# The first four head pairs of a forgetting-attention and SwiGLU kernel: q and k in two parts, gate sums by TensorE, 38 products of the identity at the start, a new order of the loads

## The chip, the cores and the metric

The kernel runs on one core of a Trainium2 chip. Its time is the device time of one execution in microseconds (us). The engines are TensorE (PE in the profile, its weight loads PEld), VectorE (DVE), ScalarE (ACT), GpSimd (POOL) and SyncE (SP), which only issues transfers (DMAs). ACT and POOL issue some transfers too.

## The reference

There are 8 batches of 8 heads, 576 positions and head size 64. The attention has a forget gate: the logarithm of a gate per position is summed along the sequence, and the difference of two such sums is added to a score. The result is reshaped to 4608 tokens of width 512 and goes through a SwiGLU block of inner width 1536.

```python
scores = scale * np.matmul(q, k.transpose(0, 1, 3, 2))
log_f = np.log(np.clip(f, 0.0001, 1.0))
cum = np.cumsum(log_f, axis=-1)
scores = np.where(causal, -1e9, scores + cum[..., :, None] - cum[..., None, :])
attn = softmax(scores)
x = (attn @ v).transpose(0, 2, 1, 3).reshape(B * S, H * D)
out = (silu(x @ w_gate) * (x @ w_val)) @ w_out
```

## The kernel before

**Pairs and halves.** Two heads make a pair, so there are 32 pairs, four to a batch. The 576 rows of a pair are nine blocks of 64; half g=0 holds row blocks 0 to 3 (columns 0 to 255 of k), half g=1 blocks 4 to 8 (all columns). The order of the halves of pairs 0 to 3 is the string HEAD: first all four g=0, then all four g=1. From pair 4 on a pair's g=1 is followed by its g=0.

**The chain of a half.** q and k of a pair are loaded in float32 (L409), cast to bf16 (L434 on ACT, L436 and L438 on DVE or POOL), transposed by TensorE into PSUM (L452) and copied to the tiles `kt` and `qz` (L464 ACT, L466 DVE). TensorE makes the scores (L498) and adds the causal mask (L502). DVE adds the gate sums `cb` and takes the row minimum in one instruction (L526, tile `t`). ACT takes the exponential with its row sum (L546, tiles `e`, `eo`). DVE makes the reciprocal (L564), POOL multiplies (L582, tile `pk`; for the first pairs ACT may, L580). For pairs 0 to 7 TensorE transposes the result (L612), which DVE or ACT copies (L617, tile `pT`); later pairs use a DMA transpose (L595). TensorE multiplies with v (L638, tile `tx`), and DVE or ACT writes the tokens to `xT` (L662).

**Gate sums.** f of all 64 heads is loaded in one transfer (L364), clipped by DVE (L366), its logarithm taken by ACT (L368) and its running sum by DVE (L369, tile `t`). A pair needs this sum with each head's row repeated over 64 partitions (`cb`). For pair 0 TensorE makes that with a matrix of ones (`select`, L393; two products of 288 columns in float32), copied by ACT (L397). For all other pairs the sums are written to device memory (L378, `cum_f`) and read back by two broadcast loads a pair (L418).

**The feed-forward part.** Tokens are taken in tiles of 256, 256, seven times 512, 256, 128, 128. A tile's gate and value products are L720, tanh L726, the two products of DVE L728 and L731, the output product L748, its copy L755 and the store L760. A unit of a 256-token tile covers two of the twelve 128-column chunks of the weights, so a tile has six units; PSUM banks are handed to units in order, so no unit overtakes an earlier one. The weights are loaded and cast by POOL's DMAs (L695 for `wg` and `wv` in pieces of 256, 256, 512, 512 columns, L699 for `wo` in three pieces).

**What sets the order.** A planner written in the kernel (class Plan) simulates all engines with a cost for each operation and a priority, and writes each engine's instructions in the resulting order; engines then run their own list in order and wait on each other. The string STARTUP is the order of the first loads: `p0` is k and q of pair 0 (on ACT's queue for pair 0, else on SP's), `f9` the gates, `c1` the two loads of pair 1's gate sums, `v04` chunk 4 of v of batch 0, `wv0` the piece of w_val that begins at chunk 0. Each of these loads waits for the landing of the one AHEAD (7) places before; a weight load waits also for the one BEHIND (6) places before and for the last weight load but one. NUDGE shifts priorities of single halves and tiles. COLD is the planner's time until which it charges TensorE double.

## Time and profile before

| | |
|---|---|
| median of 3 runs | 420.01 us (419.38 to 426.64) |
| profiled execution | 420.02 us, of which the profile's span is 418.2 us |
| PE busy | 398.1 us, 95% |
| DVE busy | 325.3 us, 78% |
| ACT busy | 311.0 us, 74% |
| POOL busy | 252.6 us, 60% |
| DMA | 72.22 MB moved, mean 173 GB/s |

How to read it: times are counted from the first instruction of the span. A row of the timeline gives start, duration, engine, line of the kernel, operation, output and input tile with their shapes, and in brackets how long the engine was idle before and what ended that. A row of the windows gives, for a stretch of time, each engine's busy time and in brackets its number of instructions, then the granted TensorE clock, the busy share of the DMA engines and the rate that they moved. A busy PE need not be a PE at its full rate: each matmul is counted with its latency, and a stream of them overlaps.

### The profile page before, as it was taken

The numbers are of one execution on the slowest core, as the hardware profiler recorded it, in microseconds if no ns is written. First come the engines' busy times: TensorE is split into PE (matmuls) and PEld (weight loads), VectorE is DVE, ScalarE is ACT, GpSimd is POOL, SyncE is SP. The second block draws the span as 40 slices with busy tenths as digits, with TensorE's granted clock in tenths as the row PEclk, the third lists the DMA queues.
The fourth block names the chain that finished last, engine by engine and source line by source line (L and its number), as shares of the span: only waits on it lengthen the run. The fifth ranks groups of instructions, "written<-read, shape, count | busy, mean of one in ns | idle before, by whom it ended". The sixth has DMA issues, their size and how long they took to land.

```text
span 418.2 us, 9999 instructions
## 1 busy us (share of the span) xinstructions
PE 398.1 (95%) x3304; PEld 231.8 (55%) x3304; DVE 325.3 (78%) x1044; ACT 311.0 (74%) x875; POOL 252.6 (60%) x460
## 2 busy tenths in 40 slices
PE   1679999999999999999999999999999999999996
PEld 1446887665555555555555555555454444447875
DVE  4589999989998979889998979898866474553532
ACT  4689999999999978888987979899886332223321
POOL 7399977999788983886795787759784000000000
PEclk9999999999999999999999999999999999999999
DMA  7999999997999999999999999979976401001111
GB/s 176 203 166 235 220 214 206 224 236 183 204 229 212 232 197 237 204 237 199 225 216 226 228 235 210 234 189 208 221 155 146 88 2 51 25 27 50 52 52 52
DMA packets 143029, 72.22 MB, mean 173 GB/s; under 512 B 117761, under 2 KB 129793, under 8 KB 142977
## 3 DMA queue, kind: packets, MB, share of 16 engines
q1 hardware_dynamic: 136804, 66.27, 73.8%
q0 software_dynamic: 5808, 4.72, 7.7%
q10 hardware_dynamic: 364, 0.59, 0.6%
q8 instruction: 26, 0.43, 0.4%
q14 instruction: 27, 0.21, 0.2%
HBM read 47.04 MB, written 9.58 MB: 135 GB/s over the span
## 4 chain that ended last, share of the span: by engine, by line
PE 77%; DMA 7%; ACT 6%; POOL 4%; DVE 3%; issue 2%; SPq 0%; POOLq 0%; DVEq 0%; ACTq 0%
PE gv L720 38%; PE gv L748 20%; PE sp L498 8%; PE tx L638 5%; DMA kf<-in_k_dram 3%; PE tx L452 3%; POOL pk L582 3%; PE gv L612 2%; DMA pT<-pk 2%; DVE t L526 2%; ACT eo L546 2%; ACT e L546 2%; PE sp L502 1%; DMA cb<-cum_f 1%; DMA cum_f<-t 1%
## 5 line engine op out<-in xcount | busy, mean ns | idle before, releaser
L526 DVE CUSTOM_DVE_ANT_0 t<-sp,cb 128x512 f32<-128x512 f32 (+7 forms) x288 | 130.9, 475 | 13.5 <-PE sp L502 5.0
L582 POOL TENSOR_SCALAR pk<-e,lr 128x128 bf16<-128x128 f32 (+3 forms) x190 | 100.1, 530 | 32.7 <-DVE lr L564 15.1
L720 PE MATMUL gv<-xT,wv 128*128 128x512 bf16 (+2 forms) x576 | 111.4, 326 | 0.0
L720 PE MATMUL gv<-xT,wg 128*128 128x512 bf16 (+2 forms) x576 | 111.3, 326 | 0.0
L728 DVE SCALAR_TENSOR_TENSOR th<-th,gv 128x512 f32<-128x512 f32 x108 | 73.9, 685 | 43.7 <-ACT th L726 43.2
L748 PE MATMUL gv<-wo,hh 128*128 128x512 bf16 (+1 forms) x444 | 107.5, 374 | 0.0
L726 ACT ACTIVATE th<-gv 128x512 f32<-128x512 f32 x108 | 64.0, 592 | 42.1 <-PE gv L720 40.3
L546 ACT ACTIVATE e<-t,tm 128x448 f32<-128x448 f32 (+4 forms) x160 | 88.5, 555 | 4.6 <-DVE tm L526 3.9
L731 DVE TENSOR_TENSOR hh<-th,gv 128x512 bf16<-128x512 f32 x108 | 73.4, 685 | 9.0 <-PE gv L720 5.5
L498 PE MATMUL sp<-kt,qz 128*128 128x448 bf16 (+6 forms) x320 | 72.8, 295 | 3.8 <-DVE tm L526 3.7
L582 POOL TENSOR_SCALAR pk<-eo,lr 128x256 bf16<-128x256 f32 (+3 forms) x128 | 67.7, 530 | 12.4 <-DVE lr L564 4.9
L546 ACT ACTIVATE eo<-t,tm 128x256 f32<-128x256 f32 (+3 forms) x128 | 71.2, 557 | 4.3 <-DVE tm L526 2.2
L720 PEld LDWEIGHTS <-wv 128*128 128x128 bf16 x576 | 49.3, 98 | 34.8
L720 PEld LDWEIGHTS <-wg 128*128 128x128 bf16 x576 | 49.2, 98 | 35.0
L748 PEld LDWEIGHTS <-hh 128*128 128x128 bf16 x444 | 39.7, 98 | 37.1
L502 PE MATMUL sp<-mask,ident 128*128 128x64 bf16 x288 | 48.2, 197 | 0.0
L755 ACT ACTIVATE ot<-gv 128x512 f32<-128x512 f32 (+1 forms) x33 | 19.1, 581 | 36.7 <-PE gv L748 34.7
L498 PEld LDWEIGHTS <-qz 128*128 128x128 bf16 x320 | 31.0, 101 | 19.8 <-DVE qz L466 1.3
L436 POOL TENSOR_SCALAR qb<-qf 72x1024 bf16<-72x1024 f32 x30 | 31.2, 1041 | 8.8 <-DMA qf<-in_q_dram 6.1
L502 PEld LDWEIGHTS <-ident 128*128 128x128 bf16 x288 | 27.2, 100 | 15.2 <-issue 3.9
L546 ACT ACTIVATION_READ_ACCUMULATOR e<-t,tm 128x1 f32 x160 | 30.7, 192 | 0.0
L638 PE MATMUL tx<-pT,vt 128*64 128x320 bf16 (+4 forms) x448 | 29.4, 266 | 0.7 <-DMA pT<-pk 0.3
(60 smaller groups left out, 379.7 us busy)
## 6 DMA issues: line engine op xcount, KB each, us to landing
out_dram<-ot SPq DMA_DIRECT2D x35, 256.0 KB
kf<-in_k_dram SPq DMA_DIRECT2D x31, 288.0 KB
qf<-in_q_dram SPq DMA_DIRECT2D x31, 288.0 KB
cb<-cum_f SPq DMA_DIRECT2D x62, 144.0 KB
vf<-in_v_dram SPq DMA_DIRECT2D x32, 256.0 KB
wo<-in_moe_w_out_dram POOLq DMA_DIRECT2D x3, 512.0 KB, 9.2
vf<-in_v_dram SPq DMA_DIRECT2D x8, 128.0 KB
wv<-in_moe_w_val_dram POOLq DMA_DIRECT2D x2, 512.0 KB, 8.3
```

The lines of the kernel that those rows point to most:

```text
L436: eng[e].tensor_scalar(dst, src, -scale, 1.0, op0=ALU.mult, op1=ALU.mult)
L498: nc.tensor.matmul(sp[:, o:o + z - a], qz[:, i, :, :].rearrange("p h r -> p (h r)"), kt[:, a:z], start=True, stop=not last or p >= MFROM)
L502: nc.tensor.matmul(sp[:, o - QB:o], ident, mask, start=False, stop=True)
L526: nc.vector.tensor_tensor_reduce(out=pl.buf(tk)[:, a:z], in0=pl.buf(sk)[:, o:o + z - a], in1=pl.buf(("cm", p))[:, i, :] if own else pl.buf ...
L546: nc.scalar.activation(pl.buf(ek)[:, :L], pl.buf(tk)[:, :L], AF.Exp, bias=pl.buf(("tm", p, g))[:, 0, i:i + 1], scale=-1.0, accum_out=pl.bu ...
L582: eng[e].tensor_scalar(dst, src, r, 1.0, op0=ALU.mult, op1=ALU.mult)
L638: nc.tensor.matmul(xo[r, 0:QB * n], vt[:, c, 2 * hp + h, :], pT[:, a:a + n, 64 * h:64 * h + 64], start=(c == 0), stop=(c == nch - 1))
L720: nc.tensor.matmul(pl.buf(bk)[:, j * n:j * n + n], wt[:, ko, fc * P:fc * P + P], xT[:, ko, x0:x0 + n], start=ko == 0, stop=ko == KD - 1)
L726: pl.op({"ACT": 487}, lambda e, u=u: nc.scalar.activation(pl.buf(("th", t, u)), pl.buf(("wg", t, u)), AF.Tanh, scale=0.5), [("wg", t, u)], ...
L728: pl.op({"DVE": 605}, lambda e, u=u: nc.vector.scalar_tensor_tensor(pl.buf(("th", t, u)), pl.buf(("th", t, u)), 1.0, pl.buf(("wg", t, u)), ...
L731: pl.op({"DVE": 605}, lambda e, u=u: nc.vector.tensor_mul(pl.buf(("hh", t, u)), pl.buf(("th", t, u)), pl.buf(("wv", t, u))), [("u", t, u), ...
L748: nc.tensor.matmul(pl.buf(bk)[:, 0:z - a], hh[:, (fc % nf) * n + ms * P:(fc % nf) * n + ms * P + P], wo[:, fc, a:z], start=fc == 0, stop=f ...
```

## The change

1. **q and k of pairs 0 to 3 in two parts.** `load_parts` loads rows 0 to 255 (part A) of k and of q for two pairs together, on 128 partitions of 4 rows each, then rows 256 to 575 (part B): k for two pairs on 128 partitions of 5 rows, q for each pair on 80 partitions of 4 rows. Part A of pairs 0 and 1 goes on ACT's queue, all else on SP's. `prepare_parts` casts each part in one instruction, transposes it and copies it to `kt` and `qz` in separate pieces for each pair (one for k, two for q). A half g=0 waits for part A only (`pair_done`, `cb_done`).
2. **Gate sums.** `select` by TensorE makes columns 0 to 255 for all four pairs, and columns 256 to 575 for pair 0. Pairs 1 to 3 load columns 256 to 575 from `cum_f`; pair 0 to 3 no longer load columns 0 to 255.
3. **38 products of the identity** with itself into a PSUM bank are TensorE's first work (`warm`).
4. **Loads and order.** STARTUP, HEAD and NUDGE are new; BEHIND goes from 6 to 4, COLD from 25000 to 6000, the buffers of v in float32 from 2 to 3, and the exponential's table load gets a bias of 1000 ns on ACT. A tile `cm` that no pair uses is gone.

```diff
-COLD = 25000
+COLD = 6000
...
+    WARM = 38
...
+    NHALF = 4
+    NSELA = 4
     NSEL = 1
+    CUT = QB * (HI[0] + 1)
...
-    BEHIND = 6
+    BEHIND = 4
...
-    STARTUP = "p0 f9 p1 c1 p3 p2 c2 v00 c3 wv0 wg2 wg0 wv2 v04 wv4 v01 v03 c4 wg4 v02 p4 wg8 wv8 v10 f0 p5 p6 c5 v14 c6 wo0 p7 wo4 v12 v13 v11 c7 wo8"
-    HEAD = "10 00 20 30 11 01 31 21"
+    STARTUP = "p0 v01 f9 wv0 p2 wg0 wv2 v00 k0 q0 q1 wg2 k2 q2 c1 c2 v02 q3 wg8 c5 c3 v04 c4 wv4 wg4 p4 wv8 v03 wo4 c0 wo0 p5 p6 c6 v14 p7 v11 v10 v12 c7 wo8 v13"
+    HEAD = "00 10 20 30 01 11 21 31"
...
-    bufs("vf", [P, H, D], F32, 2)
+    bufs("vf", [P, H, D], F32, 3)
...
+    pl.key("warm", "gv", line="w")
+    def warm(e):
+        for _ in range(WARM):
+            nc.tensor.matmul(pl.buf("warm")[:, 0:P], ident, ident, start=True, stop=True)
+    pl.op({"PE": WARM * 55}, warm, (), ["warm"], -200)
...
+    def select(p, part, a, z):
+        bk = ("cs", p, part)
...
+            nc.tensor.matmul(pl.buf(bk)[:, 0:z - a], w, pl.buf("fa")[0:BH, a:z], start=True, stop=True)
...
+    def parts(p):
+        if p % 2 == 0:
+            yield "k", "A", 0, CUT, 4, 2
+            yield "q", "A", 0, CUT, 4, 2
+            yield "k", "B", CUT, S, 5, 2
+        yield "q", "B", CUT, S, 4, 1
+
+    def load_parts(p):
...
+                for u in range(n):
+                    h0 = 2 * (hp + u)
+                    (nc.scalar if e == "ACT" else nc.sync).dma_start(
+                        out=pl.buf(fk)[m * u:m * u + m, :, 0:r * D],
+                        in_=src[b, h0:h0 + 2, a:z].rearrange("h (p r) d -> p h (r d)", r=r))
...
+        for x, a, z, sel in (("A", 0, CUT, NSELA), ("B", CUT, S, NSEL)):
+            if p < sel:
+                select(p, x, a, z)
+                continue
+            for h in range(2):
+                loads["cb", p, x, h] = pl.op({"SP": 600}, lambda e, h=h, a=a, z=z: nc.sync.dma_start(
+                    out=pl.buf(("cb", p))[64 * h:64 * h + 64, a:z],
+                    in_=cum_dram[2 * p + h:2 * p + h + 1, a:z].to_broadcast((64, z - a))),
...
+    def prepare_parts(p):
+        for name, x, a, z, r, n in parts(p):
...
+            o = pl.op({"POOL": L + 60, "ACT": L * .833 + 210, "DVE": L * .62 + 60}, cast, [fk], [bk], pr)
...
+                for j in range(r):
+                    nc.tensor.transpose(half(tk)[:, w * j:w * j + w], src[0:w, j, :], ident[0:w, 0:w])
...
+            for u in range(n):
+                for lo, hi, h in ([(0, P, None)] if name == "k" else [(0, 64, 0), (64, 128, 1)]):
+                    def evac(e, lo=lo, hi=hi, h=h, u=u, tk=tk, ok=oks[u], a=a, z=z, r=r, n=n, m=m):
...
```

In the new STARTUP `p0` and `p2` stand for part A of k and q of two pairs, `k0`, `q0` and the like for part B, and `c1` to `c3` for the columns 256 to 575 only; `c0` stands for nothing.

More of the change, by code (lines that the diff above doesn't have):

```diff
@@ L335 @@
     tiny = sb.tile([P, 2], F32)
-    one = sb.tile([BH, 2 * max(NSEL, 1), 64], F32)
-    setup({"POOL": 160 + 110 * NSEL}, lambda e: nc.gpsimd.tensor_copy(one, ident[0:BH, 0:2 * max(NSEL, 1)].unsqueeze(2).to_broadcast((BH, 2 * max(NSEL, 1), 64))),
+    one = sb.tile([BH, 2 * NSELA, 64], F32)
+    setup({"POOL": 160 + 110 * NSELA}, lambda e: nc.gpsimd.tensor_copy(one, ident[0:BH, 0:2 * NSELA].unsqueeze(2).to_broadcast((BH, 2 * NSELA, 64))),
           ["one"], -140)
@@ L531, in scores @@
                 w = [tk, ("tm", p, g)] + ([("m", p, i, a)] if two else [("m", p, i)] if last else [("m", p, i, "part")])
-                r = [sk, ("cm", p) if own else (("cb", p), 3)] + ([("m", p, i, "part")] if a and not two else [])
+                r = [sk] + ([("cm", p)] if own else cb_done(p, g)) + ([("m", p, i, "part")] if a and not two else [])
                 pl.op({"DVE": (z - a) / .96 + (142 if a and not two else 82)}, add, r, w, pr, lat=100 if p < 8 else 140, holds=[] if own else [("cb", p)])
@@ L782 @@
             line.append(loads["f", "fa", 0])
+        elif x[0] == "p" and n < NHALF:
+            line += [loads["k", n, "A"], loads["q", n, "A"]]
+        elif x[0] in "kq":
+            line.append(loads[x[0], n, "B"])
+        elif x[0] == "c" and n < NHALF:
+            line += [loads["cb", n, y, h] for y in "AB" for h in range(2) if ("cb", n, y, h) in loads]
         elif x[0] == "f" and n < NDIRECT:
```

91 lines of the change are left out of this document (71 added, 20 removed).

## The prediction

> **What bounds the kernel now.** I read the page's busy shares first, then the windows, the chain of waits over the first 20 us, and the timeline around the places that the chain names.
>
> ```profile
> PE 398.1 (95%) x3304; PEld 231.8 (55%) x3304; DVE 325.3 (78%) x1044; ACT 311.0 (74%) x875; POOL 252.6 (60%) x460
> ```
>
> PE is the engine with the least room. Where its 20 idle us lie, two tables of windows tell: the first has PE, PEld, DVE, ACT and POOL, the second PE alone.
>
> ```profile
> 0.00:10.00 10.00, 1.52 (x8) 1.24 (x9) 5.17 (x11) 4.60 (x6) 7.47 (x33) 1.00 0.70 171
> 10.00:20.00 10.00, 6.89 (x69) 5.15 (x68) 5.29 (x14) 5.45 (x14) 3.56 (x5) 1.00 0.99 213
> 20.00:30.00 10.00, 7.01 (x48) 4.45 (x47) 8.76 (x48) 9.31 (x37) 8.44 (x18) 1.00 1.17 160
> 30.00:40.00 10.00, 9.16 (x96) 6.64 (x96) 9.74 (x35) 9.41 (x26) 9.95 (x19) 1.00 1.16 228
> 40.00:50.00 10.00, 9.66 (x124) 8.01 (x122) 9.46 (x27) 9.63 (x26) 9.96 (x16) 1.00 1.17 235
> ```
>
> ```profile
> 35.00:50.00 15.00, 14.66 (x178) 1.00 1.17 238
> 50.00:60.00 10.00, 10.00 (x134) 1.00 1.04 196
> 60.00:100.00 40.00, 39.36 (x435) 1.00 0.99 221
> 100.00:300.00 200.00, 199.52 (x1600) 1.00 1.07 217
> ```
>
> From 35 us to 300 us PE is idle for 0.34 + 0 + 0.64 + 0.48 = 1.46 us. So the end follows the start: a microsecond by which the first stage is shorter is a microsecond at the end, if nothing later runs dry. In the first 20 us DVE and ACT are about half idle; from 20 us DVE, ACT and, from 30 us, POOL are over 0.84 busy, so attention can go no faster there. What it waits for first is in the chain:
>
> ```profile
> 1.38 6.10 DMA kf<-in_k_dram
> 7.60 0.83 POOL kb L438
> 8.81 3.11 DMA cum_f<-t
> 12.45 5.02 DMA cb<-cum_f
> 17.63 0.39 DVE t L526
> ```
>
> The first softmax instruction (L526) starts at 17.63 us, because pair 1 comes first in HEAD and its gate sums go to device memory and back. The timeline shows what was ready long before:
>
> ```profile
> 4.95 0.76 DVE L366 TENSOR_SCALAR t<-t 64x576 f32<-64x576 f32 x1 [1.77 <-DMA t<-in_f_dram]
> 6.45 1.35 DVE L369 TENSOR_TENSOR_SCAN t<-tiny,t 64x576 f32<-64x576 f32 x1 [0.29 <-ACT t L368]
> 9.07 2.29 PE L393 MATMUL gv<-t,one 64*128 64x288 f32 x4
> 10.43 0.40 ACT L397 COPY cb<-gv 128x288 f32<-128x288 f32 x1 [1.55 <-PE gv L393]
> 25.71 0.69 DVE L526 CUSTOM_DVE_ANT_0 t<-sp,cb 128x512 f32<-128x512 f32 x1
> 34.83 1.03 PE L720 MATMUL gv<-xT,wg 128*128 128x256 bf16 x8
> ```
>
> The gate sums of all heads are done at 6.45 + 1.35 = 7.80 us, and pair 0's first piece is in `cb` at 10.83. The four halves g=0 end where the first 512-column instruction begins, 25.71. The first feed-forward product comes at 34.83.
>
> **The change, term by term.** The sum is made against the profiled execution, 420.02 us (span 418.2 and 1.8 around it), which is the median of the runs, 420.01.
>
> *(a) First softmax instruction.* All four pairs' g=0 now take their sums from TensorE, so the 8.8 us from 8.81 to 17.63 leave the path. f is issued on SP behind one chunk of v, 128x512x4 bytes = 262 KB, which at the 213 GB/s of the second window is 1.2 us: the sums are done at 9.0 instead of 7.8. The product and its copy took 10.83 - 9.07 = 1.76 us, so L526 can start at 9.0 + 0.1 + 1.76 = 10.9 us: 6.7 us sooner. Bounds: f isn't delayed at all (7.9 us), or also shares the wire with part A of pairs 0 and 1, 524 KB or 2.4 us in its place (5.5 us). I take 6.7, since f's own queue holds only the chunk of v. Behind f's load on SP stand parts A of pairs 2 and 3; they are needed 3 to 4 us after pair 0's.
>
> *(b) What is late next: part B.* The halves g=0 took 25.71 - 17.63 = 8.1 us, so they end at 19.0. Then k0, q0 must be in. Up to and with them STARTUP holds 3.78 MB (p0 and p2 0.52 each, v 2 x 0.26, f 0.15, three weight pieces of 0.52, k0 and q0 0.49). By bytes read, at 213 GB/s after 2 us of latency, they land at 19.7; by bytes moved (a weight arrives at half its size, 3.0 MB) at 171 GB/s for 10 us and 213 after, at 16.0. Then follow a cast, transposes and a copy:
>
> ```profile
> 11.75 0.67 PE L452 MATMUL tx<-ident,kb 96*128 96x96 bf16 x6
> L438 DVE CAST kb<-kf 96x768 bf16<-96x768 f32 x1 | 0.5, 536 | 0.0
> L436 DVE TENSOR_SCALAR qb<-qf 72x1024 bf16<-72x1024 f32 x1 | 0.7, 689 | 0.0
> L466 DVE COPY qz<-tx 64x576 bf16<-64x576 bf16 x4 | 3.0, 758 | 0.8 <-PE tx L452 0.7
> L464 ACT COPY qz<-tx 64x576 bf16<-64x576 bf16 x5 | 3.1, 629 | 2.5 <-DVE tm L526 2.3 <-PE tx L452 0.2
> L397 ACT COPY cb<-gv 128x288 f32<-128x288 f32 x2 | 0.8, 398 | 2.1 <-PE gv L393 2.1
> ```
>
> 0.54 + 0.67 + 0.76 = 2.0 us, so g=1 starts between 18.0 (no loss) and 21.7 (2.7 lost). I take the middle, 1.4 given back. The weight lines of the new order stand ahead of these loads; that is what the loss pays for.
>
> *(c) More and smaller copies.* From ACT's 398 ns for 288 columns and 629 for 576, a copy costs 0.80 ns a column and 0.17 us in itself. Four pairs have 24 copies instead of 12: +2.0 us. `select` has four copies of 256 (0.37 each) and one of 320 (0.42) instead of two of 0.40: +1.1. The casts use more partitions: DVE's 536 and 689 ns give 0.60 ns an element and 0.08 us in itself; 4 x (0.54 + 0.69) = 4.9 us become 2 x (2688 elements x 0.60 ns + 5 x 0.08) = 4.0: -0.9. That is +2.2 us on DVE and ACT together, 1.1 on each, of which about half lies before 10.9 us or in the wait of (b): 0.6, between 0 and 1.1. The broadcast loads that go (64x256x4 bytes, six times) are counted in (b) and (e). The issues count too: q and k of the four pairs take 16 transfers instead of 8, 12 on SP instead of 6 and 4 on ACT instead of 2.
>
> ```profile
> 1.38 0.57 SPq L409 DMA_DIRECT2D kf<-in_k_dram  x1
> 1.17 0.67 ACTq L409 DMA_DIRECT2D qf<-in_q_dram  x1
> ```
>
> At 0.57 each SP is through v01, f and parts A of pairs 2 and 3 by 0.7 + 6 x 0.57 = 4.1 us, ahead of the wire, which needs until about 8 us for them; ACT is through its four by about 3.4 us and needs its logarithm table only near 7 us. So they are hidden; if they weren't, the six more on SP would cost 3.4 us.
>
> *(d) The 38 products.* PE is slow in this stage, as equal shapes on either side of 30 us show:
>
> ```profile
> 24.98 0.59 PE L498 MATMUL sp<-kt,qz 128*128 128x512 bf16 x1 [0.28 <-DVE tm L526]
> 25.82 0.24 PE L502 MATMUL sp<-mask,ident 128*128 128x64 bf16 x1
> 30.03 0.19 PE L502 MATMUL sp<-mask,ident 128*128 128x64 bf16 x1
> 30.63 0.38 PE L498 MATMUL sp<-kt,qz 128*128 128x512 bf16 x1 [0.19 <-DVE tm L526]
> 23.87 0.83 PE L612 MATMUL gv<-ident,pk 128*128 128x128 bf16 x6
> PE sp L498 <- DVE tm L526: 3.7, 9, 1.1
> PE tx L452 <- POOL kb L438: 8.5, 1, 8.5
> ```
>
> The granted clock reads 1.00 in every window all the same. A 128-column product takes about 0.11 us in the slow state (0.83 less a latency of about 0.25, over five), so 38 take 4.2 us, from about 1.4 to 5.6 us: under PE's wait of 8.5 us, cost 0. Part A could be cast at about 6 us, so the cover is thin; without it they would cost up to 4.2. If PE is fast afterwards, the hand-overs of two score banks between PE and DVE shorten; PE's nine waits for DVE are 3.7 us, and half of that, 1.8, is the most. DVE itself is 8.76 busy in these 10 us, so I take 0.5 (0 to 1.8). [...]
>
> *(e) The feed-forward weights.* Tile 0 cannot pass unit 1 before chunks 4 to 7 are in.
>
> ```profile
> 31.91 0.80 POOL L695 DMA_DIRECT2D wg<-in_moe_w_gate_dram  x1
> DMA to landing us min/median/max: 4.1/7.7/10.4
> 42.61 1.04 PE L720 MATMUL gv<-xT,wg 128*128 128x256 bf16 x8
> 35.00:50.00 15.00, 8.77 (x70) 6.23 (x69) 1.00 1.17 238
> ```
>
> Before, that piece (wg4) lands between 36.0 and 42.3 and is used at 42.61. Up to it the old order holds 8.80 MB, the new one 9.75 MB, since wg8 stands ahead of it: 0.95 MB or 4.0 us at 235 GB/s, less about 1.7 us because the wire, 0.70 busy in the first 10 us, is filled sooner. So it lands at 38.3 to 44.6, while its use, moved by (a) to (d), would be at 42.6 - 5.2 = 37.4: a gap of 0.9 to 7.2, middle 4.0. The last row is L720's own part of PE between 35 and 50 us, 8.77 of 14.66 busy, 0.6; the rest is attention, which goes on. On POOL the weight issues wait for landings in its own list, so its multiplies (L582) queue behind a late one, and TensorE's transposes behind those; in that case attention does not fill the gap. Lost: between 0 and 7.2 x 0.6 = 4.3. I take 1.1, about a quarter of the middle gap, because PE had only 0.34 us idle in these 15 us and so has other work queued.
>
> *New priorities after 60 us* move the order of later pairs: a gain of at most the 0.64 + 0.48 us idle there, a loss of about as much; taken as 0.
>
> Sum: -6.7 + 1.4 + 0.6 - 0.5 + 1.1 = -4.1, so 420.0 - 4.1 = 415.9 us.
>
> **The rivals.** *The whole shift is kept:* part B and the weights come in time, PE stays fast, and the 0.6 idle after 60 us goes too: 420.0 - 6.7 - 1.8 - 0.6 = 410.9. For it: the wire has room in the first 10 us. Against: it is at 0.99 to 1.17 from there on, and more bytes stand ahead of wg4.
>
> *The loads take it back (no change):* (b) and (e) at their dear ends: -6.7 + 2.7 + 0.6 - 0.5 + 4.3 = +0.4, 420.4. For it: the full wire from 10 us on.
>
> *Slower, by one piece of weight:* with BEHIND 4, wv4 can be issued only when pair 3's gate sums have landed, and wg4 when wg8 has. If wg8, wv4 and wg4 follow one another at the longest landing time, 10.4 us, from about 25 us, wg4 lands at 56, 18.6 us after 37.4; at 0.6 that costs 11.2: -6.7 + 1.4 + 0.6 - 0.5 + 11.2 = +6.0, 426.0. It decides once 0.6 of the gap exceeds the 5.2 gained, at a landing after 46.1 us. Against: median landing is 7.7 and two weight loads may overlap.
>
> **How the numbers follow.** Forecast 0.50 (412.5 to 419, 415.9), whole shift 0.18 (409.5 to 412.5), taken back 0.22 (419 to 422), slower 0.10 (422 to 430). The range 410.5 to 421.5 leaves out about a third of the whole-shift case, the slow case and a tail, 0.18. Two per cent, about what a measurement of this kernel tells from no change, is 8.4 us: below 411.6 lie most of the whole-shift case and a tail of the forecast, 0.15; above 428.4 0.04 of the slow case; 0.81 between.
>
> **What would show it.** Right: the first L526 near 10.9 us; first 512-column L526 between 18 and 22; first L720 well before 34.8, then a pause after unit 1 until wg4 lands; PE idle or slow only before that. Wrong: f landing after 7.5 us; DVE idle for over 3 us between 11 and 40; shapes of L502 at 0.24 until 30 us again (then (d) is 0); PE idle of more than 2 us after 50 us.

## The result and the profile after

The changed kernel takes 423.79 us (median of 20 runs, 421.99 to 425.32) against 420.68 us for the kernel before on the same chip (20 runs). The ratio is 1.0063, 95% interval 1.0042 to 1.0084, so it is slower by 2.6 us (1.8 to 3.5; the two medians alone lie 3.1 apart). Forecast were 415.9 us and a range of 410.5 to 421.5: the size and the sign are both wrong. The profiled execution took 424.19 us, its span is 422.4 us (before 418.2).

The page's line of busy times, after:

```profile
PE 404.9 (96%) x3286; PEld 239.0 (57%) x3334; DVE 331.0 (78%) x1061; ACT 308.2 (73%) x874; POOL 253.0 (60%) x461
```

PE is idle for 422.4 - 404.9 = 17.5 us, less than before (20.1), and yet the end is later; a busy share doesn't tell what the busy time was worth. The windows after (PE, PEld, DVE, ACT, POOL, then clock, DMA share, GB/s):

```profile
0.00:10.00 10.00, 5.45 (x46) 4.66 (x46) 4.17 (x12) 3.84 (x8) 7.63 (x34) 1.00 0.91 192
10.00:20.00 10.00, 9.56 (x42) 5.54 (x43) 4.68 (x24) 6.95 (x24) 4.39 (x7) 1.00 0.91 197
20.00:30.00 10.00, 7.99 (x69) 5.57 (x68) 9.25 (x43) 8.43 (x28) 7.54 (x17) 1.00 0.71 129
30.00:40.00 10.00, 8.38 (x71) 5.91 (x71) 8.42 (x31) 8.76 (x25) 7.08 (x13) 0.83 1.07 217
40.00:50.00 10.00, 8.03 (x86) 6.03 (x84) 8.62 (x24) 8.27 (x22) 9.59 (x16) 0.83 1.10 225
```

From 10 to 20 us PE is 9.56 busy with 42 products (before 6.89 with 69), and DVE does no more than before. From 20 to 30 the DMA share falls to 0.71 (before 1.17). From 30 to 50 every engine is less busy than before and the granted clock is 0.83. The same windows for PE alone:

```profile
35.00:50.00 15.00, 13.03 (x124) 0.80 1.10 217
50.00:60.00 10.00, 8.96 (x115) 1.00 0.92 152
60.00:100.00 40.00, 39.79 (x458) 1.00 0.93 198
100.00:300.00 200.00, 198.31 (x1557) 1.00 1.02 217
```

Between 35 and 50 us 124 products stand where 178 stood before. The part of L825 (L720 before) in that, from the windows of this line alone:

```profile
35.00:50.00 15.00, 4.56 (x28) 2.89 (x26) 0.80 1.10 217
50.00:60.00 10.00, 5.19 (x40) 3.57 (x40) 1.00 0.92 152
```

28 gate and value products against 70. After 60 us PE is full in both kernels, so there is little room to make this work up later; whether it is what costs the time, e8 tests. The start, in rows picked from a timeline of all engines:

```profile
9.15 1.35 DVE L374 TENSOR_TENSOR_SCAN t<-tiny,t 64x576 f32<-64x576 f32 x1 [0.37 <-ACT t L373]
10.98 2.07 PE L404 MATMUL gv<-t,one 64*128 64x256 f32 x4
12.64 0.42 DVE L631 CUSTOM_DVE_ANT_0 t<-sp,cb 128x256 f32<-128x256 f32 x1 [2.14 <-ACT cb L409]
13.48 1.28 ACT L651 ACT_TABLE_LOAD   x1
15.37 1.22 PE L404 MATMUL gv<-t,one 64*128 64x256 f32 x2
16.52 0.39 PE L603 MATMUL sp<-kt,qz 128*128 128x256 bf16 x1
17.43 0.42 DVE L631 CUSTOM_DVE_ANT_0 t<-sp,cb 128x256 f32<-128x256 f32 x1 [1.39 <-PE sp L607]
```

The sums are done at 10.50 us, the first softmax instruction (L631) starts at 12.64 instead of 17.63, 5.0 us sooner. Then come single waits: the exponential's table is loaded on the path (13.48, 1.28 us), and pair 1's scores (16.52, 0.39 us) stand in PE's list behind float32 products for a later pair (15.37, 1.22 us), both slow: in e5, at a granted clock of 1, the same shapes take 0.27 and 0.70. The first 512-column L631 is at 25.90, before at 25.71: the five microseconds are gone. The first two units come at 34.07 and 38.38, the third unit (number 2) at 51.98, which before began at 42.61:

```profile
34.07 1.76 PE L825 MATMUL gv<-xT,wg 128*128 128x256 bf16 x8
38.38 1.04 PE L825 MATMUL gv<-xT,wg 128*128 128x256 bf16 x8
40.09 0.79 POOL L800 DMA_DIRECT2D wg<-in_moe_w_gate_dram  x1
42.93 0.60 PE L603 MATMUL sp<-kt,qz 128*128 128x512 bf16 x2 [0.75 <-DVE tm L631]
51.04 0.38 PE L603 MATMUL sp<-kt,qz 128*128 128x512 bf16 x1 [1.38 <-DVE tm L631]
51.98 1.04 PE L825 MATMUL gv<-xT,wg 128*128 128x256 bf16 x8
```

**A measure that sorts the runs: the lag behind the plan.** The kernel's planner gives each instruction a simulated start, and every engine then runs its list in that order. So each instruction has a lag: its start in the trace less its start in the plan. DVE's 320 instructions of L631 (L526 before; the expectations call them multiplies of t) serve as milestones. The 43rd is planned at 43.49 us in the changed kernel and at 49.08 in the kernel before, and runs, in the two timelines, at:

```profile
53.03 0.62 DVE L631 CUSTOM_DVE_ANT_0 t<-sp,cb 128x448 f32<-128x448 f32 x1
```

```profile
50.53 0.62 DVE L526 CUSTOM_DVE_ANT_0 t<-sp,cb 128x448 f32<-128x448 f32 x1
```

The lags are 53.03 - 43.49 = 9.5 and 50.53 - 49.08 = 1.5 us. The 313th, planned at 312.14, runs at 322.20: 10.1. Of the changed kernel's lag 9.5 are there by the 43rd and 0.6 come in the next 270 us. The plan itself got shorter, from 415.1 us to 413.0. So 2.1 us were won in the plan and 10.1 - 4.2 = 5.9 lost behind it (4.2 is the lag of the kernel before at its 313th), net 3.8, against 4.2 in the spans.

All runs in this measure. "Plan" is the planner's own span; the lags are at the 43rd, 49th and 313th of these instructions; the span is that of the one profiled execution, so the median can differ from it by more than the usual 1.8 us around a span. Most profiled executions lie within 1.1 us of their median; those of e10 and e13 were 1.6 and 1.5 us shorter, so their lags are those of a short execution:

| kernel | plan | 43rd | 49th | 313th | span | median | ratio to before (95%) |
|---|---|---|---|---|---|---|---|
| before | 415.1 | 1.5 | 1.5 | 4.2 | 418.2 | 420.7 | |
| after | 413.0 | 9.5 | 9.5 | 10.1 | 422.4 | 423.8 | 1.0063 (1.0042 to 1.0084) |
| e1_no_products | 413.0 | 7.1 | 7.1 | 8.2 | 420.6 | 423.0 | 1.0054 (1.0024 to 1.0085) |
| e2_exp_table | 413.0 | 6.4 | 9.6 | 10.4 | 422.7 | 423.8 | 1.0071 (1.0046 to 1.0097) |
| e3_weights_early | 413.0 | 9.5 | 9.4 | 10.1 | 422.4 | 424.2 | 1.0104 (1.0066 to 1.0141) |
| e4_own_q_buffers | 413.0 | 9.1 | 9.0 | 9.7 | 422.0 | 424.0 | 1.0077 (1.0040 to 1.0113) |
| e5_fast_pe | 413.0 | 8.4 | 8.6 | 9.2 | 421.5 | 423.7 | 1.0043 (1.0015 to 1.0070) |
| e6_cold | 415.5 | 1.1 | 5.1 | 6.8 | 422.5 | 423.9 | 1.0038 (1.0003 to 1.0074) |
| e7_before_fast_pe | 415.1 | 6.1 | 6.2 | 8.4 | 422.4 | 424.2 | 1.0071 (1.0041 to 1.0100) |
| e8_weights_k2 | 416.7 | 2.1 | 2.7 | 4.6 | 421.0 | 423.5 | 1.0060 (1.0025 to 1.0094) |
| e9_weights_q3 | 415.7 | 5.6 | 5.8 | 7.8 | 422.5 | 423.5 | 1.0048 (1.0013 to 1.0084) |
| e10_weights_q3_own | 415.7 | 3.4 | 3.8 | 5.2 | 419.9 | 423.4 | 1.0044 (1.0012 to 1.0075) |
| e11_all | 413.0 | 8.5 | 8.7 | 9.3 | 421.6 | 423.6 | 1.0085 (1.0061 to 1.0110) |
| e12_exp_weights | 413.0 | 9.2 | 9.1 | 9.7 | 422.1 | 424.0 | 1.0089 (1.0056 to 1.0122) |
| e13_replanned | 413.8 | 2.6 | 2.7 | 4.1 | 417.4 | 420.8 | 0.9980 (0.9948 to 1.0011) |
| e14_fast_idle | 413.0 | 8.5 | 8.4 | 9.0 | 421.4 | 423.2 | 1.0065 (1.0031 to 1.0100) |
| e15_replanned_fast | 413.8 | 5.5 | 5.6 | 6.7 | 419.6 | 421.9 | 1.0015 (0.9983 to 1.0046) |

Plan and last lag add up to the span within 1.1 us in every row (after: 413.0 + 10.1 = 423.1; e6: 415.5 + 6.8 = 422.3; e13: 413.8 + 4.1 = 417.9); as the lag is counted from the same plan, this says no more than that little is won or lost behind the 313th. And the lag of the 49th is that of the 313th but for 0.6 to 2.8 us: what these lists lose in their first 55 us they keep.

### The profile page after: what moved, and what is told of

The parts are those of the page before. It is cut to its first block, busy times and chain, and to the rows that moved or that the text cites. A ratio compares the mean times of both kernels' runs of the same rounds, so it can differ in the third digit from the quotient of the medians.

```text
span 422.4 us, 10030 instructions
## 1 busy us (share of the span) xinstructions
PE 404.9 (96%) x3286; PEld 239.0 (57%) x3334; DVE 331.0 (78%) x1061; ACT 308.2 (73%) x874; POOL 253.0 (60%) x461
## 4 chain that ended last, share of the span: by engine, by line
PE 86%; issue 1%; DVE 0%; ACT 0%; DVEq 0%
PE gv L825 43%; PE gv L853 22%; PE sp L603 9%; PE tx L743 6%; PE tx L476 3%; PE gv L717 2%; PE sp L607 2%; DVE t L631 0%; ACT ot L860 0%; DVE tm L631 0%; DVEq L631 0%
## 5 line engine op out<-in xcount | busy, mean ns | idle before, releaser
L631 DVE CUSTOM_DVE_ANT_0 t<-sp,cb 128x320 f32<-128x320 f32 (+7 forms) x288 | 131.4, 475 | 16.7 <-PE sp L607 7.3
L687 POOL TENSOR_SCALAR pk<-e,lr 128x512 bf16<-128x512 f32 (+1 forms) x192 | 101.0, 530 | 50.0 <-DVE lr L669 24.1
L825 PE MATMUL gv<-xT,wv 128*128 128x512 bf16 (+2 forms) x568 | 110.7, 327 | 0.4
L825 PE MATMUL gv<-xT,wg 128*128 128x512 bf16 (+2 forms) x557 | 109.4, 326 | 0.9
L853 PE MATMUL gv<-wo,hh 128*128 128x512 bf16 (+1 forms) x424 | 103.7, 373 | 0.9
L603 PE MATMUL sp<-kt,qz 128*128 128x512 bf16 (+7 forms) x319 | 73.5, 294 | 5.4 <-DVE tm L631 4.0
L687 POOL TENSOR_SCALAR pk<-eo,lr 128x256 bf16<-128x256 f32 (+1 forms) x126 | 66.8, 530 | 14.2 <-DVE lr L669 9.6
L825 PEld LDWEIGHTS <-wv 128*128 128x128 bf16 x576 | 49.8, 98 | 35.5 <-issue 0.3
L825 PEld LDWEIGHTS <-wg 128*128 128x128 bf16 x576 | 49.2, 98 | 34.5
L607 PE MATMUL sp<-mask,ident 128*128 128x64 bf16 x288 | 48.3, 197 | 0.0
L860 ACT ACTIVATE ot<-gv 128x512 f32<-128x512 f32 (+1 forms) x31 | 17.9, 579 | 33.0 <-PE gv L853 33.0
L607 PEld LDWEIGHTS <-ident 128*128 128x128 bf16 x288 | 27.2, 100 | 14.5 <-issue 3.0
L460 POOL TENSOR_SCALAR qb<-qf 72x1024 bf16<-72x1024 f32 x28 | 29.1, 1039 | 3.2 <-DVE tm L631 1.8
```

What stands on the lines that cost most here:

```text
L460: eng[e].tensor_scalar(dst, src, -scale, 1.0, op0=ALU.mult, op1=ALU.mult)
L603: nc.tensor.matmul(sp[:, o:o + z - a], qz[:, i, :, :].rearrange("p h r -> p (h r)"), kt[:, a:z], start=True, stop=not last or p >= MFROM)
L607: nc.tensor.matmul(sp[:, o - QB:o], ident, mask, start=False, stop=True)
L631: nc.vector.tensor_tensor_reduce(out=pl.buf(tk)[:, a:z], in0=pl.buf(sk)[:, o:o + z - a], in1=pl.buf(("cm", p))[:, i, :] if own else pl.buf ...
L687: eng[e].tensor_scalar(dst, src, r, 1.0, op0=ALU.mult, op1=ALU.mult)
L825: nc.tensor.matmul(pl.buf(bk)[:, j * n:j * n + n], wt[:, ko, fc * P:fc * P + P], xT[:, ko, x0:x0 + n], start=ko == 0, stop=ko == KD - 1)
```

## The experiments

**e1 to e4: one cause at a time.** The first four took one suspected cause each off the changed kernel's own lists. Their expectations use the letters A to D for theories with a single cause.

e1, without the 38 products:

```diff
-        for _ in range(WARM):
+        for _ in range(0):
```

> The changed kernel without its 38 products; every engine's list is otherwise the same. Theory A (the products end at 5.65 us and leave PE slow until 27.4 us, so they do nothing): 423.8 us as the changed kernel, ratio to before 1.005 to 1.008, equal shapes still slow (0.26 us for a mask product) until about 27 us. Rival (they buy speed in the first scores, or they hold PE up): the ratio moves by over 0.003 either way.

1.0054 against 1.0063 for the changed kernel: the intervals overlap almost wholly, so no worth of the 38 products is to be seen either way. The lag of e1's profiled execution is smaller all the same, 7.1 at the 43rd: the granted clock fell to 0.5 once in it, at 42.33 us, where it fell twice in that of the changed kernel.

e2, the exponential's table load ahead of ACT's first copy of `cb`:

```diff
...
+        last = wrote((("qz", 1), "A"))[-1]
+        place(wrote("exp")[0], last)
+        place(last, wrote("exp")[0])
...
```

> The changed kernel with the exponential's table load put back ahead of the first exponential, where ACT waits for the first gate sums (10.99 to 12.23 us); lists otherwise the same. Theory B (the table load of 1.28 us at 13.48 us lies on the path of the first halves, and the end follows): first exponential at about 13.4 instead of 14.77 us, 1.0 to 1.3 us off the end, 422.6 us. Rival C (the start is not what costs; the feed-forward weights are): the first exponential is earlier and the end stays within 0.5 us of 423.8.

The time did not fall (1.0071). But the lag did, to 6.4 at the 43rd, and was back at 9.6 by the 49th. PE's timeline of e2 has the reason:

```profile
47.93 0.38 PE L603 MATMUL sp<-kt,qz 128*128 128x512 bf16 x1 [1.28 <-DVE tm L631]
...
50.68 1.89 PE L825 MATMUL gv<-xT,wg 128*128 128x256 bf16 x8 [1.66 <-DMA wg<-in_moe_w_gate_dram]
...
53.71 1.04 PE L825 MATMUL gv<-xT,wv 128*128 128x256 bf16 x8
```

PE came to unit 2 at 49.0 us, stood 1.66 us for its weights, and then ran it in 1.89 us instead of 1.04, at half clock (the granted clock is 0.5 from 50.30 to 53.71 us). One wait had hidden the next.

e3, the pieces wv4 and wg4 issued ahead of wg8:

```diff
...
+        for w in ("wv", "wg"):
+            place(loads[w, 4], loads["wg", 8])
...
```

> The changed kernel with POOL's two issues of the pieces wv4 and wg4 moved ahead of wg8 in POOL's list (26.5 us instead of 36.25 and 40.09); all else in its place. Theory C (unit 2 of the first token tile cannot start before wg4 lands at 49.5 us, and PE runs out of work between 40 and 52 us): wg4 lands before 42 us, unit 2 starts at 43 to 45 us instead of 51.98, 2 to 4 us off the end, 420 to 422 us. Rival (PE's order has other waits there, DVE's list above all): unit 2 starts no sooner than 48 us and the end stays within 0.7 us of 423.8.

The weights of unit 2 lay there at 38.05 us, 11.4 us sooner than after (49.46), and unit 2 began at 51.89, after at 51.98. The time did not fall (1.0104). So the weights alone are not what holds unit 2: it has its place in PE's list, behind scores that wait for DVE.

e4, own places for the second parts of q of pairs 2 and 3:

```diff
+    own = {("qf", p, "B"): pl.pools["ot"][p - 2][:, :].rearrange("p (h x) -> p h x", h=2) for p in (2, 3)}
...
-                        out=pl.buf(fk)[m * u:m * u + m, :, 0:r * D],
+                        out=(own[fk] if fk in own else pl.buf(fk))[m * u:m * u + m, :, 0:r * D],
...
```

> The changed kernel with part B of q of pairs 2 and 3 landing in tiles of their own, so that SP's list no longer stands from 15.8 to 22.7 us behind the cast of q of pair 0. Theory D (that wait of 6.8 us starves the wire between 17 and 26 us and makes all later loads late): the DMA share between 20 and 25 us rises from 0.64 to about 1.0, wg4 lands 2 us sooner, 1 to 2 us off the end, 422 to 423 us. Rival C (the weight issues stand behind multiplies in POOL's list, whatever SP does): the DMA share rises, but wv4 is still issued at about 36 us and the end stays within 0.5 us of 423.8.

SP's list no longer stands for the buffer of q (6.8 us in the changed kernel), the DMA share between 20 and 25 us rises from 0.64 to 0.92 (from 20 to 30 us it is 0.70, after 0.71), and the time does not fall (1.0077).

**e5 to e7: the clock and the plan.** COLD tells the planner until when PE is slow; the change set it from 25000 to 6000 ns. In the changed kernel PE was slow until 27.4 us: a mask product (L607) takes 0.26 us at 26.02 and 0.19 at 27.56.

e5, products of the identity ahead of each attention operation, into the bank which that operation fills anew:

```diff
-        for _ in range(WARM):
+        for _ in range(56):
...
+            if o.eng == "PE" and o.start < 42000 and key[0] != "warm" and key[0][0] not in ("wg", "wv"):
+                for _ in range(12 if o.start < 9000 else 4):
+                    nc.tensor.matmul(pl.buf(key[0])[:, 0:P], ident, ident, start=True, stop=True)
             o.fn(o.eng)
```

> The changed kernel with its lists as they are, 56 products of the identity at the start instead of 38, and more such products ahead of each of TensorE's attention operations: 12 ahead of those planned before 9 us, 4 ahead of those planned before 42 us, none ahead of the gate and value products. Each goes into the bank that the operation behind it fills anew. Theory E (the order was planned for a TensorE at full speed from 6 us on, and it was slow until 27.4 us and at a granted clock of 0.5 in two rows between 34 and 48 us): the granted clock is 1 from 6 to 10 us on without a 0.5 row, the mask's products take 0.19 us throughout, the first 512-column multiply of t comes at 22 to 23.5 us (25.90 in the changed kernel), the first gate and value unit before 32 us (34.07), unit 2 before 49 us (51.98), and the time falls to 420 to 421.5. Rival R (the lists of VectorE, ScalarE and SyncE hold the start back at any clock): the clock is mended, the multiply comes no sooner than 25 us and the time stays within 0.8 us of 423.8. If the clock is not mended, the run tells neither.

The granted clock is 1 from 4.9 us to the end. The first 512-column L631 comes at 23.97 us, between the two expectations, unit 2 still after 50 us, the lag at the 43rd is 8.4 and the time 1.0043, within rival R's bounds. So in this run a fast PE takes little of the lag away. What the slow clock costs by itself that doesn't tell, because the added products wait for the same bank as the operation behind them and then delay it: at 49.68 us, after a wait of 1.33 us for DVE, four of them come first and the scores begin 0.22 us behind.

e6, one constant back to its value before:

```diff
-COLD = 6000
+COLD = 25000
```

> One line of the change undone: the constant COLD, up to which the planner in the kernel counts TensorE as slow, is 25000 again as in the kernel before, so that the lists are planned anew; halves of q and k, gate sums by TensorE, 38 products and the order of loads stay. The planner's own span is 415.5 us with it, against 413.0 for the changed kernel and 415.1 for the kernel before. Theory E (a wrong clock in the plan costs the time): lists that fit the clock, unit 2 at or before 48 us, and a time of 420.5 to 422. Rival R (halves and early sums themselves cost it): 423 to 425.

The lag at the 43rd falls from 9.5 to 1.1: made for a slow PE, the lists fit the chip that far. The time misses theory E all the same: 423.9 us, and 1.0038, which can't be told from the changed kernel's 1.0063. By the table there are two reasons. The plan is 2.5 us longer, and the lag jumps by 4.0 until the 49th. There PE's wait on the weights of unit 2 is to be seen, and behind it the granted clock is 0.5 from 49.85 to 53.27 us:

```profile
48.88 1.05 PE L825 MATMUL gv<-xT,wg 128*128 128x256 bf16 x8 [2.23 <-DMA wg<-in_moe_w_gate_dram]
```

e7, the kernel before with the products of e5:

```diff
+        new = 56
...
+                for _ in range(new or (12 if o.start < 9000 else 4)):
+                    nc.tensor.matmul(pl.buf(key[0])[:, 0:P], ident, ident, start=True, stop=True)
+                new = 0
```

> The kernel before with its lists as they are, 56 products of the identity ahead of its first TensorE operation and more ahead of the attention operations as in the run above (12 ahead of those planned before 9 us, 4 before 42 us). It tells whether a fast TensorE is worth something by itself at the start. If the slow clock binds in the kernel before as well: clock 1 from 12 us on, first 512-column multiply of t at 23.5 to 25 (25.71), time 418 to 419.5. If its order is fitted to a slow TensorE (its lists and its loads bind): 420 to 421, within 0.7 of the kernel before.

It is 3.0 us slower (1.0071), outside both expectations. The granted clock is 1 from 4.33 us on, but for 17.98 to 21.39 us, and still the lag at the 43rd is 6.1 (1.5 before). These lists fit a slow PE, and here the products put between their operations cost more than the faster PE gave.

**e8 to e10: the weights early in list and load at once.** COLD 25000, the planner made to place unit 2 early.

```diff
-    STARTUP = "p0 v01 f9 wv0 p2 wg0 wv2 v00 k0 q0 q1 wg2 k2 q2 c1 c2 v02 q3 wg8 c5 c3 v04 c4 wv4 wg4 p4 wv8 v03 wo4 ...
+    STARTUP = "p0 v01 f9 wv0 p2 wg0 wv2 v00 k0 q0 q1 wg2 wv4 wg4 k2 q2 c1 c2 v02 q3 wg8 c5 c3 v04 c4 p4 wv8 v03 wo4 ...
```

> The run e6 (COLD back at 25000) with the pieces of 512 columns of the gate and value weights (wv4, wg4) ahead of the second parts of pair 2 in the order of loads, planned anew: the planner issues them at 17.4 and 21.6 us and puts unit 2 at 34.1 us in TensorE's list (42.5 in the changed kernel, 45.2 in e6). The planner's span is 416.7 us, 1.2 longer than that of e6 and 1.6 longer than that of the kernel before. Theory F (what is lost is gate and value work between 35 and 52 us: unit 2 is late by its place in the list and by its weights together, and TensorE, full from 60 us on, never gives it back): unit 2 starts by 41 us, at least 60 gate and value products are done at 50 us (70 before, 32 in the changed kernel and in e5), and the time is 419.5 to 421.5. Rival G (TensorE's work is only moved: attention comes later by as much, and the halves cost it anyway): the products are there by 50 us and the time stays at 423 to 425.

e9 has `... k2 q2 c1 c2 v02 wv4 wg4 q3 c5 c3 v04 c4 p4 wv8 wg8 v03 ...` in that string.

> As the run above, with wv4 and wg4 ahead of the second part of pair 3's q and the last gate piece wg8 moved behind wv8: planned issues 22.3, 23.6 and 33.0 us, unit 2 planned at 34.8 us, planner's span 415.7 us. Theory F: unit 2 by 42 us, at least 56 gate and value products by 50 us, time 420 to 422. Rival G: 423 to 425.

e10 is e9 with the edit of e4.

> As e9, and the second parts of q of pairs 2 and 3 land in the output tiles, which are empty until 60 us, as in e4, so that SyncE's list does not stand for a buffer of q. If SyncE's standing list holds the start back once the weights are early, the share of the DMA engines between 20 and 25 us rises and the time falls by 0.5 to 1 against e9; if not, it is within 0.5 of e9.

Theory F, that the late unit 2 is the loss, falls. The windows of L825 in e8:

```profile
35.00:50.00 15.00, 9.37 (x73) 6.48 (x72) 1.00 0.98 208
50.00:60.00 10.00, 0.00 (x0) 0.00 (x0) 1.00 1.21 210
```

The gate and value products of 35 to 50 us are there (73, before 70), and then there are none for the next 10 us, since all 96 products of tile 0 are done by 50 us and the first of tile 1 comes at 62.99: the work was only moved, as rival G said. The times are 1.0060, 1.0048 and 1.0044. In e10 the DMA share between 20 and 25 us rises from 0.71 to 0.93 and the time stays within 0.5 us of e9, so SP's list isn't what holds the start back there. What the three show in the table is that the lag at the 43rd can be small (e8 2.1, e10 3.4, but e9 5.6) and that their plans are longer than that of the kernel before (416.7 and 415.7).

**e11, e12: several causes at once on the changed kernel's lists.** e11 joins the edits of e2 to e5, e12 those of e2 and e3.

> The changed kernel's lists with all four covers at once: the extra products of e5 (fast TensorE), the exponential's table early (e2), wv4 and wg4 issued ahead of wg8 (e3), and q's second parts of pairs 2 and 3 in the output tiles (e4). Theory S (barriers in series: every operation's lag behind the plan is made before 55 us by several waits that stand one behind the other, is kept to the end by lists of fixed order, and taking one away leaves the next): the lag of the multiplies of t behind the plan, 9.5 us at the 43rd of them and 10.1 at the 313th in the changed kernel, falls to 6 or less, and the time to 420 to 422. Rival R (the halves cost it whatever the start does): 423 to 425.

> The changed kernel's lists with the covers of e2 and e3 together: the exponential's table early, and wv4 and wg4 issued ahead of wg8. Alone neither gained: in e2 TensorE came to unit 2 at 49 us with a lag of 6.4 us and then stood 1.7 us for its weights and ran it at half speed; in e3 the weights lay there from 38 us on and TensorE came to unit 2 at 51.9 us with a lag of 9.5. Theory S: both together keep the smaller lag, 6 to 7.5 us to the end, and the time is 420.5 to 422.5, if the granted clock is not at 0.5 between 31 and 48 us (where it is, 2 to 3 us of lag come back). Rival R: 423 to 425.

Both missed: 1.0085 and 1.0089. In e11 the lag is 1.4 at the first of these instructions, jumps by 2 us from the 3rd to the 5th and again from the 37th to the 39th, and grows in small steps between, much as in e5. In e12 it is 5.8 at the 37th instruction, as hoped, and 9.2 at the 43rd, and between the two the clock is at 0.5, from 42.81 to 49.63 us. e2 has almost the same lists and a clock of 1 from 29.82 to 50.30 us, and there the lag is still 6.4 at the 43rd; so the clock has most likely taken back what was won. PE's windows in e12, in the steps of 3.41 us in which its granted clock changes:

```profile
35.98:39.39 3.41, 3.30 (x39) 1.00 1.20 220
39.39:42.81 3.42, 1.81 (x12) 1.00 1.20 231
42.81:46.22 3.41, 2.81 (x22) 0.50 0.94 177
46.22:49.63 3.41, 3.40 (x36) 0.50 0.84 202
49.63:53.05 3.42, 2.37 (x30) 1.00 1.10 192
```

**e13 to e15: a short plan and a small lag.** e13 is e10 with STARTUP, HEAD and NUDGE found anew by trial, for a short plan:

```diff
-    STARTUP = "p0 v01 f9 wv0 p2 wg0 wv2 v00 k0 q0 q1 wg2 k2 q2 c1 c2 v02 wv4 wg4 q3 c5 c3 v04 c4 p4 wv8 wg8 v03 wo4 c0 ...
-    HEAD = "00 10 20 30 01 11 21 31"
+    STARTUP = "p0 v01 f9 wv0 p2 wg0 wv2 v00 k0 k2 q0 q1 wg2 v02 c2 q2 c1 wg4 wv4 q3 c3 c4 c5 v03 v04 p4 wg8 wv8 c0 v14 ...
+    HEAD = "00 20 10 30 01 11 31 21"
...
```

> The kernel of e10 (halves of q and k, gate sums by TensorE, 38 products, COLD 25000, own places for q's second parts) with the three strings that steer the planner (order of loads, order of the first units, nudges of the due times) found anew by trial with the planner's own span as the aim, under the condition that each weight piece is issued 13 us before its first use in the plan. The planner's span is 413.8 us; it was 415.7 for e10, 413.0 for the changed kernel, 415.1 for the kernel before. Theory S (time is the planner's span and the lag that the waits of the first 55 us make): with the lag of e8 and e10 (2 to 3.5 us at the 43rd multiply of t, 4.5 to 5.2 at the 313th) the span is 418 to 419.5 and the time 420 to 421.5, 2 to 3 below e10 and level with the kernel before. Rival R (halves and early sums cost it by themselves): 423 to 425.

The time came out as theory S has it: median 420.75, ratio 0.9980 (0.9948 to 1.0011), level with the kernel before. The lag is 2.6 at the 43rd and 4.1 at the 313th, and the span of 417.4 us lies below the expected 418, the profiled execution being a short one. So a kernel with the halves and the early sums can be as fast as the one before, and rival R falls. That they cost nothing by themselves isn't shown, since the strings were found anew as well. Its windows:

```profile
10.00:20.00 10.00, 10.00 (x58) 6.86 (x59) 7.20 (x36) 7.58 (x27) 5.71 (x11) 0.50 1.21 253
20.00:30.00 10.00, 8.04 (x68) 4.74 (x66) 9.36 (x40) 9.62 (x34) 8.59 (x18) 0.72 1.04 189
30.00:40.00 10.00, 8.14 (x70) 5.95 (x70) 8.39 (x29) 8.18 (x27) 7.61 (x13) 0.83 1.17 224
40.00:50.00 10.00, 10.00 (x141) 8.77 (x140) 9.94 (x27) 9.32 (x22) 9.91 (x16) 1.00 1.18 202
```

DVE has 7.20 busy us from 10 to 20 (after 4.68, before 5.29), at a granted clock of 0.50. The first 512-column softmax instruction is 2.4 us sooner than before, unit 2 begins 2.7 us sooner (before 42.61), and the 43rd of the softmax instructions, planned at 47.71, runs at 50.30 (L632 and L826 are the lines that L631 and L825 are after):

```profile
23.34 0.69 DVE L632 CUSTOM_DVE_ANT_0 t<-sp,cb 128x512 f32<-128x512 f32 x1
39.96 1.04 PE L826 MATMUL gv<-xT,wg 128*128 128x256 bf16 x8
50.30 0.18 DVE L632 CUSTOM_DVE_ANT_0 t<-sp,cb 128x64 f32<-128x64 f32 x1
```

e14 is e12 with added products in a bank that has stood empty longest, so that they run while PE waits:

```diff
...
+                many = 5 if o.start < 24000 else 8 if o.writes[0][0] == "sp" else 0
+                if best and best[0] < o.start - 400:
+                    for _ in range(many):
+                        nc.tensor.matmul(pl.buf(best[1])[:, 0:P], ident, ident, start=True, stop=True)
```

> The kernel of e12 (lists of the changed kernel, exponential's table and weights early) with 56 products at the start and products of the identity ahead of attention operations as in e5, but 5 ahead of each that is planned before 24 us and 8 ahead of each score operation planned from there to 42 us, and written into a bank that has stood empty longest, so that they run while TensorE waits. Theory S: the granted clock stays at 1 from 6 us on, the lag at the 43rd multiply of t is 4 to 6.5 us (9.2 in e12, 8.5 in e5 and e11), and the time is 420 to 421.5. Rival R: 423 to 425.

Missed: 423.19 us, 1.0065, with the clock at 1 from 7.3 us on. The lag is 5.4 at the 25th instruction (6.3 after) and 8.5 at the 43rd; that the added products stand in the way between the two is likely, not shown. What the changed kernel's lists would do on a PE that is fast without added work stays open, and no run here can show it.

e15 is e13 with the added products of e14.

> The kernel of e13 with the products of e14. If the slow clock still costs the kernel of e13 something, the time falls by 0.5 to 1.5 us against e13; if its lists, which were planned for a slow TensorE until 25 us, already hold the cost, it stays within 0.6 of e13.

It is 1.1 us slower by its median than e13, neither of the two that were expected; the lag of 5.5 against 2.6 says that here, too, the added products cost more than the clock gives.

## Why the prediction was wrong, step by step

**The frame held, the stage did not.** "A microsecond by which the first stage is shorter is a microsecond at the end, if nothing later runs dry" fits the lags, which stay from 55 us on. The working moved the start, and took for granted that everything behind it follows at its old pace. It did not, in two places. The first 512-column instruction was to come near 20.4 us (25.71 - 5.3) and came at 25.90: that is the whole gain gone, 1.7 of it in (a) and the rest in (b). From there to the 43rd instruction another 2.3 us are lost against the kernel before (25.90 against 25.71 first, then 53.03 against 50.53). That is more than half of the 4.2 us by which the span is longer, and the forecast had only (e) for it.

**(a) First softmax instruction: 6.7 us sooner forecast, 5.0 measured.** f came in time (5.95 us, "wrong" was set at 7.5). 1.5 us more than forecast went before the sums were done: ACT's logarithm (8.44) stood behind a cast of k that waited for its load until 6.57 and a copy to `kt`. I had costed f's load and not what is ahead of the logarithm in ACT's list.

**(b) The halves g=0: the failed step.** I gave them the 8.1 us that they took before, from the first L526 to the first 512-column one. They took 25.90 - 12.64 = 13.3. Before, the stage began at 17.63, and by then PE had made pair 0's sums, five of the eight groups of transposes and one pair's scores, while the softmax had to wait anyway. Now the float32 products for pairs 2 and 3 and for pair 0's second part (1.22, 1.22 and 1.43 us), the transposes for pairs 2 and 3 and the scores of pairs 1 to 3 lie inside the stage, in one list, and PE is slow in it: a mask product (L607) takes 0.26 us up to 26.02 us, and 0.19 from 27.56. Stage durations were carried over although the work in the stage had changed. That isn't the whole of it. In e6, e8, e9, e10 and e13, which do the same operations in lists made with COLD at 25000, the stage takes 10.4 to 10.5 us (e6: 12.79 to 23.21, with the granted clock at 0.5 from 8.89 to 22.54). So of the 5.2 us too many about 2.8 go with the order of the lists, and about 2.4 remain, with the work that is now inside. Part B, the loss that I did cost (1.4), was not the limit. Its first k was in at 13.94 us, where k and q had been forecast for 16.0 to 19.7 (the later with 2 us of latency; in the kernel before the busy share of the DMA engines is 0.00 up to 1.5 us, 0.33 from there to 2.0 and 0.70 to 2.5), and PE came to its transposes only at 20.98; DVE's cast of the first q, at 22.21, did not wait for a load either:

```profile
13.94 0.72 POOL L543 CAST kb<-kf 128x640 bf16<-128x640 f32 x1 [1.64 <-DMA kf<-in_k_dram]
20.98 0.69 PE L555 MATMUL tx<-ident,kb 128*128 128x128 bf16 x5 [0.97 <-DVE kt L570]
```

**(c) Copies: about right.** By tiles, up to 45 us, the copies to `kt`, `qz` and `cb` on DVE and ACT rose by 2.9 us (forecast 2.0 + 1.1), and the casts on these two engines fell by 1.6 (forecast 0.9), so the term is +1.3 instead of +2.2, too small a difference to matter.

**(d) The products: -0.5 forecast, nothing measured (e1).** The 38 took 4.24 us (4.2 forecast) and ended at 5.65 us, PE then waited 1.6 us for its first part, and shapes of L607 took 0.26 us until 26 us: the sign that I had named for a gain of 0. That PE would be fast behind them was an assumption, which no row of the kernel before showed. Of the ten profiled kernels with 38 products the clock rose between 5.1 and 6.2 us in eight (e2, e4, e6, e8, e9, e10, e12, e13), and fell back 3.4 us later in each; in the changed kernel and in e3 it did not rise before 24, as in e1, which has no products. In the eight, PE is busy for 2.85 to 3.42 us in the 3.41 us ahead of the rise, and for 0.66 to 1.02 in the 3.41 us behind it. In the changed kernel, in windows of this length counted back from the first change of its clock (27.39), the products lie across two with 2.08 and 2.15 us busy (e3: 2.39 and 2.36). But 3.41 and 3.42 us busy from 10.32 to 17.15 did not raise the clock of the changed kernel either, so what raises it is not shown. The products went with a rise in most of these kernels, and where the clock rose it did not stay up behind them.

**(e) The weights: 1.1 forecast, and the wrong question.** wg4 landed at 49.46, beyond the end that I gave (44.6) and beyond the 46.1 from which the slower rival was to decide. So that rival's condition came true, but e3 shows that its mechanism does not carry the loss: with the weights at 38.05 the time was no shorter. The waits for earlier landings that I had put into it, and that the description of the kernel names for AHEAD and BEHIND, belong to the planner's model; on the chip the two issues stood at their places in POOL's list (36.25 and 40.09 us), and e3 only moved them there (26.23 and 27.04, the second long before the first had landed at 33.87). Unit 2's place in the list had been made from the weights' planned landing (42.24 us, with unit 2 planned at 42.46), so the two were late together. The gate and value work is also no loss in itself (e8).

**What I left out: the plan.** COLD went from 25000 to 6000. I described that line and never put a price on it, though I had measured that PE is slow until 30 us. e6 shows what it did to the order: with the constant of before the lag at the 43rd is 1.1 us instead of 9.5. That a plan's error is not a loss of the same size is as plain there: e6's plan is 2.5 us longer and runs into the next wait. Shown by the runs is that the lag is made in the first 55 us and kept, and that with another plan (e13: COLD 25000, other strings, own places for q) the kernel is level with the one before. Which of these edits does it isn't shown: e6 has COLD alone and stays at 1.0038, and e10 has all but the strings and stays at 1.0044. How the 9.5 us divide between the clock, the table and the list places isn't settled either, since taking away one of them left the others standing (e2, e3, e5, e12).

One rival was not followed up, though the runs have numbers for it: the clock that falls back to 0.5 in the middle of the start. A window of 3.41 us at 0.5 lowers the mean granted clock of an execution by 0.5 x 3.41 / 420 = 0.004, so such windows can be counted in each; in the profiled executions they all lie before 54 us. Of the executions of the kernel before that were measured beside e1 to e15, 105 have none (median 420.3 us) and 20 have one (423.6). Of e1's twelve, 3 have none (421.6), 4 one (422.1), 3 two (424.1) and 2 three (425.1). So such windows go with about 0.5 to 3 us each, and without them e1 is 1.2 us from the kernel before, by three executions. Whether the fallen clock makes the loss, or whether the waits that make the loss also let the clock fall, no run separates.

## What to carry to other kernels

Where each engine runs a fixed list, price a change by the lists: compare a milestone's planned start with its traced start, and look for the first place where the lag grows; a single cover that leaves the time alone may only have uncovered the next wait. A duration read from a stage holds only for the work and the clock of that stage. Where a planner carries a constant about the machine, a change of that constant is part of the change, and it is to be held against the trace like any other term.

## What the runs showed of the hardware that was not expected

Cut into steps of 3.41 us, the first 60 us of each of the 17 profiled kernels have a granted clock of 1.00 or 0.50 in every step and no value between. In the changed kernel it falls twice to 0.5 after it had risen at 27.39, while PE has work and is idle for no more than 0.75 us at a time:

```profile
27.39:30.80 3.41, 2.52 (x26) 1.00 0.83 135
30.80:34.21 3.41, 1.83 (x24) 1.00 1.04 227
34.21:37.63 3.42, 3.42 (x18) 0.50 1.05 226
37.63:41.04 3.41, 3.41 (x43) 1.00 1.11 187
41.04:44.45 3.41, 1.91 (x18) 1.00 1.17 246
44.45:47.87 3.42, 3.42 (x32) 0.50 1.13 216
```

Each 0.5 window follows one in which PE was busy for 1.83 or 1.91 of 3.41 us. In the first 62 us of all 17 profiled kernels there are 22 such falls, each after a window with 0.66 to 2.24 us busy; no window with more was followed by one, and some between 1.75 and 2.24 were not either. The clock rose only after windows with 2.85 us or more. So in the changed kernel 1.58 and 1.50 us of idle time in 3.41, in pieces, came ahead of its two falls, and 1.51 us, from 47.87 to 51.28, was not followed by one. e5 and e14, which keep every window above 2.24 us, have no row at 0.5 up to 62 us after the first rise:

```profile
7.28:10.69 3.41, 2.42 (x37) 1.00 1.22 209
10.69:14.11 3.42, 3.34 (x31) 1.00 1.19 261
14.11:17.52 3.41, 3.41 (x47) 1.00 1.14 252
```

(e14.) And a row of 1.00 does not say that PE is fast: until 27 us the changed kernel's rows read 1.00 while equal shapes took 0.26 instead of 0.19 us. The first entry in the trace's record of the clock is at 27.39 us there, and at 29.92 in the kernel before.
